# One more half chunk with the first expert layer in 44 instead of 48 short matmuls per expert

## The chip, the cores and the metric

The program runs on one core of a Trainium2 chip. The metric is the device time of one execution in microseconds (us). The engines of the core are named as the profile names them: PE (TensorE, matmuls), PEld (PE's weight loads, which overlap its matmuls), DVE (VectorE), ACT (ScalarE), POOL (GpSimd) and SP (SyncE, which here only issues DMAs). Each engine works through its own queue of instructions in order and waits for others on semaphores. PSUM is the memory that PE writes to, in eight banks.

## What is computed

A gated linear attention over 4 batches, 8 heads, 768 steps, 48 numbers per head, and behind it a mixture of 4 experts on every token (all experts are used, weighted by given probabilities):

```python
f = 1.0 / (1.0 + np.exp(-f_logit))
for t in range(S):
    state = f[:, :, t, :, None] * state + np.einsum('bhd,bhe->bhde', k[:, :, t], v[:, :, t])
    y[:, :, t] = np.einsum('bhd,bhde->bhe', q[:, :, t], state)
# x: y with the heads side by side, 3072 tokens x 384
p = domain_probs / (domain_probs.sum(-1, keepdims=True) + 1e-09)
for e in range(E):                       # 4 experts
    h = np.maximum(x @ w1[e], 0.0)       # 384 -> 1024, the first expert layer
    out += p[:, e:e + 1] * (h @ w2[e])   # 1024 -> 384, the second
```

## The kernel before

The sequence is cut into six chunks, 0 to 5, of 128 steps. In a chunk, attention is done batch by batch: from f come the gates (`gate1`, `gate2`, two activations on ACT for two batches at once from chunk 1 on), from these PE makes cumulative sums (`cs`, `pe_cs`), ACT their exponentials, DVE or POOL multiply them with q and k, a transpose follows, then PE makes the masked scores (`at`) and the output (`y`). The output is scaled by the probabilities and transposed by a DMA into `xs`, the input of the experts.

The experts of a chunk work on halves: half 0 is batches 0 and 1, half 1 batches 2 and 3, 256 tokens each. A group (chunk, half, pair) is one half through two experts. Its first layer is done in one of two ways:

- plainly (`mm_hs`): per expert 24 matmuls with 256 columns each (as long as 48 with 128 columns), 8 row blocks of 128 hidden units by 3 blocks of the 384 inputs. Four tiles of 128 x 512 leave PSUM through a ReLU on ACT or DVE (`relu_s`);
- by a Winograd form of Strassen's scheme (`l1_unit`, `mm_l1`): over two of the three input blocks, 2 x 2 blocks are multiplied with 7 products instead of 8, 28 matmuls of 128 columns, and 16 more for the third input block: 44. It needs sums of weight blocks (`u_sums`, five per expert, made once, kept in buffers that the loads of f, q, k and the gates used before) and of input blocks (`x_sum`, four per group, kept in a buffer of the loads of v), and three partial results are copied out of PSUM by ACT (`copy_l1`) and added in when a quarter of the hidden units is finished (`ev_l1`, three of four on DVE). One PSUM bank collects the four quarters one after another, so PE's next step into it waits for the eviction before.

The set `LOW` names the groups that go the second way: before the change all four of chunk 5. The second layer always goes by such a scheme: each group has seven steps of 8 matmuls with 192 columns (`mm_p`, "step 1" to "step 7" below), whose results are added to the output tile by DVE (`ev_p`). `s_sum` makes the sums of hidden blocks for them on DVE or POOL.

What stands where is not decided by the code's order. Each operation is entered with `P.add`, which gives it the next entry of the table `RANKS`: a number that is its place in the program, and at some entries a letter that fixes its engine (A for ACT, D for DVE, P for POOL). All operations are then written out in the order of these numbers, so every engine's queue, SP's queue of DMAs too, follows the table. Buffers are given out in the same order.

Two gates on loads matter below: the f of chunk 1 is loaded in two parts, and the second (`load`, `w_gate`) is issued only when a certain weight load has landed. SP issues loads, transposes and stores in one queue.

Of the kernel before, what the change touches and what calls it, by code (L numbers as in the profile page):

```python
# [143 lines left out]
def kernel(  # L144
# [957 lines left out]
    for c in range(C):  # L1102
# [30 lines left out]
        elif c > 1:  # L1133
            if c == C - 1:
                for e in sorted({2 * p + el for _, _, p in LOW for el in range(2)}):
                    u_sums(e)
# [23 lines left out]


PRINT = None
LOW = {(5, 0, 0), (5, 0, 1), (5, 1, 0), (5, 1, 1)}
BLOCKED = {(0, 1), (1, 1), (1, 3)}
YP, RP = 17, 50
B1, S1, B2, S2 = -10, 4, -2, 6
# [38 lines left out]
```

## Time and profile before

| what | value |
|---|---|
| three runs | 287.25, 286.94, 285.03 us; median 286.94 |
| the profiled execution | 285.82 us, of which the span of its instructions is 284.1 us |
| busy share of the span: PE, DVE, POOL, ACT | 97%, 73%, 65%, 63% |
| DMA | 41.88 MB, mean 147 GB/s |
| granted clock of PE | 1.00 in all but the very end |

The span runs from the first instruction to the last. The execution's time holds about 1.7 us more than the span, for what lies around it. "Busy" of PE counts matmuls from their start to a modelled end, and neighbours overlap, so that 97% does not yet say that PE never waits; the list of waits and the distances between starts do.

### The profile page before, as it was taken

The numbers are of one execution on the slowest core, as the hardware profiler recorded it, in microseconds if no ns is written. First come the engines' busy times: TensorE is split into PE (matmuls) and PEld (weight loads), VectorE is DVE, ScalarE is ACT, GpSimd is POOL, SyncE is SP. The second block draws the span as 40 slices with busy tenths as digits, with TensorE's granted clock in tenths as the row PEclk, the third lists the DMA queues.
The fourth block names the chain that finished last, engine by engine and source line by source line (L and its number), as shares of the span: only waits on it lengthen the run. The fifth ranks groups of instructions, "written<-read, shape, count | busy, mean of one in ns | idle before, by whom it ended". The sixth has DMA issues, their size and how long they took to land.

```text
span 284.1 us, 8015 instructions
## 1 busy us (share of the span) xinstructions
PE 276.0 (97%) x3228; PEld 241.2 (85%) x3228; DVE 208.7 (73%) x437; ACT 178.2 (63%) x350; POOL 185.3 (65%) x197
## 2 busy tenths in 40 slices
PE   6889999999999999999999999999999999999995
PEld 4678565668788999999998999999999899999995
DVE  5695487797779587769887786686765687857683
ACT  5668235647898848686866867769367456556420
POOL 5799353706699878667729955695656545793761
PEclk9999999999999999999999999999999999999999
DMA  6999999999988999999999999996547015201003
GB/s 156 189 195 205 208 195 200 184 216 181 162 150 159 198 164 208 204 168 184 194 175 207 194 179 218 184 166 124 111 82 160 30 31 76 67 0 59 2 2 111
DMA packets 153688, 41.88 MB, mean 147 GB/s; under 512 B 144028, under 2 KB 152860, under 8 KB 153652
## 3 DMA queue, kind: packets, MB, share of 16 engines
q1 hardware_dynamic: 142404, 34.66, 65.1%
q0 software_dynamic: 11248, 6.72, 16.8%
q8 instruction: 25, 0.41, 0.6%
q14 instruction: 11, 0.09, 0.1%
HBM read 31.51 MB, written 4.72 MB: 128 GB/s over the span
## 4 chain that ended last, share of the span: by engine, by line
PE 84%; DMA 9%; POOL 4%; ACT 1%; DVE 1%; issue 0%; ACTq 0%; POOLq 0%
PE ps_m L646 29%; PE ps_m L531 26%; PE ps_m L574 7%; DMA w_sb<-in_moe_w_dram 7%; PE ps_m L514 6%; PE ps_m L499 4%; PE ps_m L654 2%; DMA f<-in_f_logit_dram 2%; PE ps_m L437 2%; POOL w_sb L312 2%; PE ps_m L464 1%; PE ps_m L460 1%; PE ps_m L347 1%; PE ps_m L470 1%; POOL AT L441 1%; PE ps_m L362 1%
## 5 line engine op out<-in xcount | busy, mean ns | idle before, releaser
L531 PE MATMUL ps_m<-x,w_sb 128*128 128x256 bf16 x672 | 84.3, 273 | 0.0
L531 PEld LDWEIGHTS <-w_sb 128*128 128x128 bf16 x672 | 63.6, 98 | 7.1
L595 ACT ACTIVATE h<-ps_m 128x512 bf16<-128x512 f32 x82 | 46.8, 600 | 24.1 <-PE ps_m L531 23.9
L646 PEld LDWEIGHTS <-S 128*128 128x128 bf16 x576 | 48.2, 98 | 0.8
L673 DVE TENSOR_TENSOR o<-ps_m,o 128x192 f32<-128x192 f32 x91 | 31.1, 353 | 19.1 <-PE ps_m L646 17.3
L646 PEld LDWEIGHTS <-h 128*128 128x128 bf16 x432 | 36.2, 98 | 0.8
L610 POOL TENSOR_TENSOR S<-h 128x1024 bf16<-128x1024 bf16 x14 | 29.7, 2124 | 10.3 <-DVE S L610 6.3
L499 PE MATMUL ps_m<-x,w_sb 128*128 128x128 bf16 (+2 forms) x264 | 35.1, 282 | 0.0
L420 ACT ACTIVATE yb<-ps_m,pn 128x384 bf16<-128x384 f32 x55 | 29.4, 586 | 8.5 <-PE ps_m L464 5.6
L397 POOL TENSOR_TENSOR qk<-q,e 128x384 bf16<-128x384 f32 x18 | 21.6, 1201 | 12.5 <-DVE f L549 3.9
L646 PE MATMUL ps_m<-ts_sb,S 128*128 128x192 bf16 x288 | 29.3, 246 | 0.0
L646 PE MATMUL ps_m<-w_sb,h 128*128 128x192 bf16 x288 | 29.2, 246 | 0.0
L646 PE MATMUL ps_m<-w_sb,S 128*128 128x192 bf16 x288 | 28.7, 246 | 0.0
L499 PEld LDWEIGHTS <-w_sb 128*128 128x128 bf16 x264 | 21.6, 98 | 8.1
L593 DVE TENSOR_SCALAR h<-ps_m 128x512 bf16<-128x512 f32 x30 | 20.6, 688 | 9.6 <-PE ps_m L531 8.5
L453 DVE TENSOR_TENSOR AT<-ps_m,mask 128x512 bf16<-128x512 f32 x40 | 25.6, 682 | 2.1 <-PE ps_m L437 2.0
L510 ACT ACTIVATE h<-ps_m 128x512 bf16<-128x512 f32 x33 | 19.1, 595 | 12.2 <-PE ps_m L499 11.8
L380 ACT ACTIVATE e<-ps_m 128x384 f32<-128x384 f32 x40 | 23.6, 708 | 3.2 <-PE ps_m L347 1.4
L610 POOL TENSOR_TENSOR S<-h,S 128x1024 bf16<-128x1024 bf16 x10 | 21.2, 2124 | 4.5 <-DVE o L673 2.5
L514 PE MATMUL ps_m<-w_sb,h 128*128 128x384 bf16 x128 | 23.9, 326 | 0.0
L585 DVE CUSTOM_DVE_ANT_0 h<-ps_m,QK 128x512 bf16<-128x512 f32 x24 | 16.0, 686 | 5.1 <-PE ps_m L574 1.9
L588 ACT COPY QK<-ps_m 128x512 f32<-128x512 f32 x24 | 13.8, 588 | 8.1 <-PE ps_m L574 5.2
(140 smaller groups left out, 523.3 us busy)
## 6 DMA issues: line engine op xcount, KB each, us to landing
out_dram<-o SPq DMA_DIRECT2D x23, 192.0 KB, 2.5
w_sb<-in_moe_w_dram POOLq DMA_DIRECT2D x5, 768.0 KB, 15.2
k<-in_k_dram SPq DMA_DIRECT2D x10, 384.0 KB, 5.1
q<-in_q_dram SPq DMA_DIRECT2D x10, 384.0 KB, 5.0
v<-in_v_dram SPq DMA_DIRECT2D x10, 384.0 KB, 5.1
f<-in_f_logit_dram SPq DMA_DIRECT2D x9, 384.0 KB, 5.8
w_sb<-in_moe_w_dram POOLq DMA_DIRECT2D x6, 384.0 KB, 8.2
f<-in_f_logit_dram SPq DMA_DIRECT2D x6, 192.0 KB, 4.4
```

The costliest lines, as they stand in the source:

```text
L380: nc.scalar.activation(out=o, in_=i, func=AF.Exp, scale=1.0 if j else -1.0)
L397: return engines[eng].tensor_tensor(out=tl("qk", c, b)[:, j, :, 0:D].rearrange("t (i r) d -> t i r d", r=2), in0=tl("qk"[j], c, b // 2)[:, ...
L420: nc.scalar.activation(out=ys, in_=y, func=AF.Copy, scale=pe)
L453: nc.vector.tensor_tensor(out=tl("AT", c, b)[:, r].rearrange("s i t -> s (i t)"), in0=tl("A", c, b, r).rearrange("s i t -> s (i t)"), in1= ...
L499: nc.tensor.matmul(out=hp(c, e, fc, n0, n1, nf)[:, f], lhsT=w1_sb[:, e, kk, (fc + f) * 128:(fc + f + 1) * 128], rhs=tl("xT", c)[:, kk, n0: ...
L514: nc.tensor.matmul(out=tl("op", c, e, nt)[:, 0:Din], lhsT=tl("h", c, e, half_of(c, nt * T))[:, fc, nt * T:(nt + 1) * T], rhs=w2_sb[:, e, f ...
L531: nc.tensor.matmul(out=out_[:, f], lhsT=w1_sb[:, e, kk, (fc + f) * 128:(fc + f + 1) * 128], rhs=tl("xs", c, hf, p)[:, el, kk, :], start=(k ...
L593: nc.vector.tensor_relu(out=dst, in_=tl("hp", c, hf, p, el, fc))
L595: nc.scalar.activation(out=dst, in_=tl("hp", c, hf, p, el, fc), func=AF.Relu)
L610: return engines[eng].tensor_tensor(out=o, in0=in0, in1=in1, op=op)
L646: nc.tensor.matmul(out=out_, lhsT=lhs[:, f, :], rhs=rhs[:, f, :], start=(first and el == 0 and f == 0), stop=(el == 1 and f == KH - 1), sk ...
L673: nc.vector.tensor_tensor(out=o, in0=src, in1=o, op=ALU.add)
```

## The change

The groups (4, 1, 0) and (4, 1, 1), the second half of chunk 4 through both pairs of experts, join `LOW`. With them the twenty sums of weight blocks are entered at chunk 4 instead of chunk 5 (`u_sums` is called in the chunk that first needs it, and left out where the sum exists). And the table `RANKS` is another one, since 32 operations are added and every number may move: from the second expert of chunk 0 on, order and engines differ in most of the program.

```diff
 RANKS = (
-    "0 9 14 1 5 18 3 27 2 21 33 48 19 40 24 52 30 61 36 71 42 84 55 95 63 109 74 121 80 137 88 151 97 163 169 106 165 114 184 "
+    "0 9 14 1 5 18 3 27 2 21 33 48 19 40 24 52 30 61 36 71 42 84 55 95 63 109 74 121 80 137 88 151 97 163 204 106 168 114 218 "
...
         elif c > 1:
-            if c == C - 1:
-                for e in sorted({2 * p + el for _, _, p in LOW for el in range(2)}):
-                    u_sums(e)
+            for e in sorted({2 * p + el for g, _, p in LOW if g == c for el in range(2)} - {e for e, _ in usums}):
+                u_sums(e)
             for hf in range(2):
                 for p in range(NPR):
                     zip_groups((c, hf, p), prev)
...
-LOW = {(5, 0, 0), (5, 0, 1), (5, 1, 0), (5, 1, 1)}
+LOW = {(4, 1, 0), (4, 1, 1), (5, 0, 0), (5, 0, 1), (5, 1, 0), (5, 1, 1)}
```

Three places where the queues differ. The change has one line more in `RANKS`, so L499 of before is L500 after it, and so on.

PE, at the first cumulative sums of chunk 1 (the matmuls from `gp` and `Ub`; the rows on `w_sb` and `x` are the first layer of chunk 0, those on `S` are the second layer of its expert 1). Before:

```order
L654 LDWEIGHTS S_770
L654 MATMUL ps_m_711<-w_sb,S_770 128x192
L499 LDWEIGHTS w_sb
L499 MATMUL ps_m_807<-x_372,w_sb 128x512
L499 LDWEIGHTS w_sb
L499 MATMUL ps_m_807<-x_372,w_sb 128x512
L499 LDWEIGHTS w_sb
L499 MATMUL ps_m_807<-x_372,w_sb 128x512
L347 LDWEIGHTS Ub
L347 MATMUL ps_m_815<-gp_88,Ub 128x384
L347 LDWEIGHTS Ub
L347 MATMUL ps_m_818<-gp_88,Ub 128x384
```

and after the change:

```order
L500 LDWEIGHTS w_sb
L500 MATMUL ps_m_800<-x_372,w_sb 128x512
L348 LDWEIGHTS Ub
L348 MATMUL ps_m_806<-gp_88,Ub 128x384
L655 LDWEIGHTS S_681
L655 MATMUL ps_m_707<-w_sb,S_681 128x192
```

The step of the second layer that ends in the first two rows of before (step 7 of expert 1, eight matmuls) has moved behind the first cumulative sum; the other work ahead of it has the same length.

ACT, some 20 us later: the gates of a later chunk (`f<-f` is `gate1`, `gp<-f` is `gate2`), exponentials (`e`) and the ReLUs of chunk 1's first layer (`h`). Before:

```order
L334 ACTIVATE f_878<-f_878 128x768
L380 ACTIVATE e_102<-ps_m_1066 128x2x4x48
L380 ACTIVATE e_102<-ps_m_1066 128x384
L380 ACTIVATE e_104<-ps_m_1041 128x2x4x48
L380 ACTIVATE e_104<-ps_m_1041 128x384
L510 ACTIVATE h_1118<-ps_m_1081 128x2x256
L342 ACTIVATE gp_88<-f_878 128x16x48
```

and after:

```order
L335 ACTIVATE f_925<-f_925 128x768
L343 ACTIVATE gp_88<-f_925 128x16x48
L381 ACTIVATE e_104<-ps_m_1093 128x2x4x48
L381 ACTIVATE e_104<-ps_m_1093 128x384
L335 ACTIVATE f_1072<-f_1072 128x768
L511 ACTIVATE h_1150<-ps_m_1143 128x2x256
L511 ACTIVATE h_1102<-ps_m_1129 128x2x256
```

A gate of chunk 3 (`f_1072`) now stands ahead of chunk 1's ReLUs; its load is the fifth that SP issues counted from the f of chunk 2, where before the fifth was a load of k.

SP, its last stores (`o` is the output tile, 128 rows by 384 or 192 columns). Before:

```order
L677 DMA out_dram<-o_4218 128x384 x2
L677 DMA out_dram<-o_4681 128x384
L677 DMA out_dram<-o_4926 128x384
L677 DMA out_dram<-o_4681 128x384
L677 DMA out_dram<-o_4926 128x192 x2
```

and after:

```order
L678 DMA out_dram<-o_5059 128x192
L678 DMA out_dram<-o_4814 128x384
L678 DMA out_dram<-o_5059 128x192
L678 DMA out_dram<-o_5059 128x384
L678 DMA out_dram<-o_4814 128x384
```

The last store is now one of 384 columns, 192 KB, instead of one of 192 columns.

117 rows, old and new, of the table RANKS are left out of this document.

## The prediction

> **What bounds the kernel now.** I read the page first, then the list of what PE waited for, then the chain that ended last. From the page, the span and the busy shares:
>
> ```profile
> span 284.1 us, 8015 instructions
> PE 276.0 (97%) x3228; PEld 241.2 (85%) x3228; DVE 208.7 (73%) x437; ACT 178.2 (63%) x350; POOL 185.3 (65%) x197
> ```
>
> PE is busy nearly throughout. Whether it ever waits is in the list of waits on PE, over the whole span (us in total, times, longest):
>
> ```profile
> engine line waited for: us in total, times, longest us
> PE ps_m L1156 <- DVE S L192: 1.5, 1, 1.5
> PE ps_m L437 <- DVE QK L288: 1.3, 3, 0.6
> PE ps_m L464 <- POOL AT L441: 0.7, 1, 0.7
> PE ps_m L351 <- POOL mask L220: 0.7, 1, 0.7
> PE ps_m L347 <- ACT gp L342: 0.7, 1, 0.7
> ```
>
> All five belong to the start and to chunk 0's end. The same list for 50 us onward has no row at all: for 230 us PE waits for nobody. So the end is the moment of the last wait, at L347, plus the matmuls behind it, plus the tail. The chain of work shows what sets that moment (start, length):
>
> ```profile
> 41.45 5.70 DMA f<-in_f_logit_dram
> 47.24 0.85 ACT f L334
> 48.11 0.85 ACT gp L342
> ```
>
> and PE's timeline shows it standing there:
>
> ```profile
> 47.51 0.81 PE L499 MATMUL ps_m<-x,w_sb 128*128 128x512 bf16 x3
> 49.01 0.48 PE L347 MATMUL ps_m<-gp,Ub 128*128 128x384 bf16 x2 [0.68 <-ACT gp L342]
> ```
>
> Chunk 1's f is issued at 41.45 behind a weight load and lands at 47.15; two activations follow, and PE's first cumulative sum begins at 49.01. Nothing in the change makes that load earlier: SP's loads up to it and POOL's issues of weights stand in the same order.
>
> **What the half itself saves.** Two stretches of the chain give the price of a matmul of either kind, and one that of a step of the second layer:
>
> ```profile
> 88.64 0.66 PE ps_m L654 x8
> 89.47 2.62 PE ps_m L531 x24
> 256.68 2.68 PE ps_m L574 x48
> ```
>
> Plain first layer: 2.62 / 24 = 0.1092 us per matmul, 24 per expert, 2.62 us. The other form: 2.68 / 48 = 0.0558 us, 44 per expert, 2.46 us. Four expert passes (two pairs of two) change: 4 x (2.62 - 2.46) = **0.66 us less PE work**, in 284.
>
> The Trainium skill says otherwise of such short matmuls: TensorE: Matmul & The Clock Gate, section "Back-to-back issue gap", gives about 81 ns per matmul for a sustained stream of weight load and matmul with 128 columns. By it four passes would take 4 x 44 x 0.081 = 14.3 us, some 4 us more than now (an estimate from that page). The row above has a weight load per matmul as well and 55.8 ns; the trace decides.
>
> **What the new order takes back.** In the new order, step 7 of expert 1 (eight matmuls, 0.66 us by the row of x8) stands behind the first cumulative sum instead of ahead of it; the other work ahead is equal in length. PE thus arrives at the sum 0.66 us sooner, and waits for the same gate until 49.0: its wait grows from 0.68 to about 1.35. From 49.01 it works without a wait until its last step (quoted below) has gone through at 280.17 + 0.66 = 280.83, 231.8 us; after the change it still has 231.8 - 0.66 + 0.66 to do from there. The saving and the moved step cancel: **net 0.0**. If PE were late by then for another reason, up to 1.3 us of it would be covered by the same wait.
>
> **What else moves, and its cover.** The half's 16 evictions of 512 columns become 28, and eight sums of input blocks are new; the twenty weight sums are the same, only sooner. Their rows by group:
>
> ```profile
> L595 ACT ACTIVATE h<-ps_m 128x512 bf16<-128x512 f32 x82 | 46.8, 600 | 24.1 <-PE ps_m L531 23.9
> L593 DVE TENSOR_SCALAR h<-ps_m 128x512 bf16<-128x512 f32 x30 | 20.6, 688 | 9.6 <-PE ps_m L531 8.5
> L585 DVE CUSTOM_DVE_ANT_0 h<-ps_m,QK 128x512 bf16<-128x512 f32 x24 | 16.0, 686 | 5.1 <-PE ps_m L574 1.9
> L588 ACT COPY QK<-ps_m 128x512 f32<-128x512 f32 x24 | 13.8, 588 | 8.1 <-PE ps_m L574 5.2
> L561 POOL TENSOR_TENSOR v<-x,v 128x256 bf16<-128x256 bf16 x5 | 3.4, 670 | 1.6 <-DVE S L610 1.4
> ```
>
> The half had 12 evictions on ACT and 4 on DVE, 12 x 0.60 + 4 x 0.69 = 10.0 us; it gets 16 on ACT (12 copies, 4 ReLUs) and 12 on DVE, 12 x 0.59 + 4 x 0.60 + 12 x 0.69 = 17.7 us, and 8 x 0.67 = 5.4 us of input sums if all were POOL's. Spread over some 30 us they lie beside PE's matmuls:
>
> ```profile
> core 0: us, PE busy (x) PEld busy (x) DVE busy (x) ACT busy (x) POOL busy (x), PEclk, DMA share, GB/s
> 49.00:55.00 6.00, 6.00 (x48) 4.02 (x48) 4.43 (x9) 3.76 (x7) 4.30 (x6) 1.00 1.16 189
> 200.00:215.00 15.00, 15.00 (x188) 13.97 (x186) 10.67 (x24) 8.95 (x20) 9.01 (x10) 1.00 0.50 106
> 215.00:230.00 15.00, 15.00 (x178) 13.84 (x176) 9.85 (x20) 9.27 (x20) 9.19 (x7) 1.00 0.31 73
> ```
>
> In the last two of these stretches DVE has 9.5 us free in 30 and ACT 11.8, against some 5.5 and 2.3 more. The weight sums need the buffers of chunk 5's f, q and k, so SP loads these up to 25 us sooner; over the last third the DMA engines are half idle or more (0.50 and 0.31 above). I take nothing for it. If the cover were gone, each eviction that is late costs PE up to its own 0.69.
>
> The real risk is in tight pairs: two steps of the second layer into one PSUM bank with little between them. After a step's last matmul, the eviction and the next start need, by the end of the program,
>
> ```profile
> 280.17 0.82 PE L646 MATMUL ps_m<-w_sb,h 128*128 128x192 bf16 x8
> 281.03 0.36 DVE L673 TENSOR_TENSOR o<-ps_m,o 128x192 f32<-128x192 f32 x1 [0.30 <-PE ps_m L646]
> ```
>
> 0.16 (the end beyond its 0.66) + 0.04 + 0.36, and 0.05 until PE goes on (48.96 to 49.01 above): 0.61 us. Adding up the PE steps that stand between such pairs, the closest before the change had 1.11 us; after it five have less, the closest (chunk 2, half 0, pair 0, steps 7 and 4) 0.81. All clear 0.61 if DVE is free at that moment; if a 0.69 operation is just running, up to 0.5 us is lost. Bounds: 0 and 5 x 0.5 = 2.5; I take **0.3**, near the lower end, since the chains of other kinds (scores to output, ReLU to sums) keep their closest distances (2.16 and 2.17 us for scores to output).
>
> The last store: the two last ones (96 KB) landed in the first of these rows' time, all five of the end in the second:
>
> ```profile
> DMA to landing us min/median/max: 1.6/1.6/1.6
> ...
> DMA to landing us min/median/max: 1.6/1.8/1.9
> ```
>
> A 192 KB store at the very end lands 1.9 - 1.6 = **0.3 us** later; bounds 0 and, by the page's medians of 2.5 and 1.6, 0.9.
>
> **Sum.** 284.1 - 0.66 + 0.66 + 0.3 + 0.3 = 284.7 of span. The profiled execution took 285.82, 1.72 above its span, so 286.4; the median of the runs shown is 286.94, 1.1 above that, which would give 287.5. I take the middle, **287.0**.
>
> **The rivals.**
> (a) The saving stays: the load of f happens to land sooner, or PE is late enough to use the wait. Then 0.66 less, 286.3. For it: only that DMA landings vary. Against: the same queue ahead of it.
> (b) ACT is held up by chunk 3's gate. It now stands ahead of four ReLUs of chunk 1, and waits for the load that SP issues as fifth after the f of chunk 2's start. That place in the old queue was a load of k:
>
> ```profile
> 62.69 1.61 SPq L301 DMA_DIRECT2D k<-in_k_dram  x1
> ...
> f<-in_f_logit_dram SPq DMA_DIRECT2D x9, 384.0 KB, 5.8
> ```
>
> so it lands near 62.7 + 5.8 = 68.5. Summed from 49.0, PE's second layer wants the first of these ReLUs at 73.6 and the fourth at 74.3 (an estimate: the new order's steps at the rates above); a gate and four ReLUs take 0.85 + 4 x 0.60 + 0.2 = 3.45. It decides from a landing at about 70.8 on, and every us beyond costs PE one: three late would make 290. For it: the load moved ahead into the busiest stretch for DMA (a share of 1.16 from 49 to 55, above). Against: 2.3 us of room.
> (c) DVE, which by the letters of `RANKS` gets 14 operations more (the half's 12 evictions at 0.69 among them, some 9 us in all), is the engine that the tight pairs run into; a dozen pairs have under 1.4 us, at up to 0.5 each some 3 us more, 290. Against: 9.5 us of 30 free even in the changed half.
> (d) Matmuls of 128 columns slow down when the half runs amid chunk 4's other work, toward the 81 ns named above: some 4 us more, 291. Chunk 5's rows say no.
> (e) The change does not do what it says: excluded as far as the order goes, 176 matmuls of 128 columns stand where 96 of 256 stood.
>
> **How the numbers follow.** A measurement of this kernel tells about 1%, 2.9 us, from no change; its own runs spread over 2.2. Forecast 0.66, (a) 0.12, (b) 0.08, (c) 0.12, (d) 0.01, 0.01 for a gain by luck in the start. Only (b), (c) and (d) can reach slower by over 1%, and half of (c)'s smaller forms stay below; with something for delays in a reordered program that I don't see, slower 0.18. Faster by over 1% has no source: all waits of PE together are 4.9 us and lie where the order is nearly unchanged; 0.02. Within 1%: 0.80. The range runs from 285.0, the lowest run shown, which (a) would reach on a good day, to 290.0, where (b) and (c) at their middle end.
>
> **What would show it.** In the list of waits on PE, L348 (the sum's new line) should stand with 1.2 to 1.5 us instead of 0.7, starting near 48.35 and ending at 49.0; behind 50 us there should be no row, or rows of a few tenths at L647. The groups should show 352 + 176 matmuls of 128 columns at 219 ns each and 56 ns apart, and 576 instead of 672 at the plain form. The last store should land 1.8 to 1.9 after its issue. I am wrong if PE's first sum of chunk 1 starts elsewhere than at 49.0, or if waits for DVE or ACT of more than 1 us in all stand behind it.

## The result

In 22 runs of each kernel the median is 288.47 us after the change (286.97 to 293.79) and 286.31 us before (285.03 to 291.46). The ratio of after to before is 1.0077, with a 95% interval of 1.0049 to 1.0105: slower by 0.8%, less than the 1% that the prediction called a difference. Here and below the ratios leave out single slow runs (three of after, 292.24 to 293.79, one of before, 291.46, and one of 997.30 in "banks kept"), while the medians are over all runs. The forecast was 287.0, the range 285.0 to 290.0. The profiled execution took 288.16 us, with a span of 286.4; before it was 285.82 and 284.1. These 2.3 us of span can be found one by one.

From the page of the kernel after, the span and the busy shares:

```profile
span 286.4 us, 8192 instructions
PE 275.4 (96%) x3308; PEld 240.9 (84%) x3308; DVE 216.3 (76%) x451; ACT 180.3 (63%) x355; POOL 183.0 (64%) x198
```

PE is busy 0.6 us less, as the shorter half should have it, and the span is longer all the same. What PE waited for, from 45 us to the end (us in total, times, longest); before there was one row here, 0.7 us at the first cumulative sum:

```profile
PE ps_m L348 <- ACT gp L343: 2.1, 2, 1.8
PE ps_m L647 <- ACT e L381: 0.6, 1, 0.6
PE ps_m L532 <- DMA x<-yb: 0.2, 1, 0.2
```

PE's timeline at these places, with the matmuls ahead of each (start, length):

```profile
49.21 0.32 PE L348 MATMUL ps_m<-gp,Ub 128*128 128x384 bf16 x1 [1.81 <-ACT gp L343]
...
66.83 0.82 PE L500 MATMUL ps_m<-x,w_sb 128*128 128x256 bf16 x6
67.98 0.32 PE L348 MATMUL ps_m<-gp,Ub 128*128 128x384 bf16 x1 [0.34 <-ACT gp L343]
...
115.27 1.24 PE L647 MATMUL ps_m<-ts_sb,S 128*128 128x192 bf16 x13
116.71 1.49 PE L532 MATMUL ps_m<-x,w_sb 128*128 128x256 bf16 x12 [0.21 <-DMA x<-yb]
...
138.47 0.82 PE L532 MATMUL ps_m<-x,w_sb 128*128 128x256 bf16 x6
139.93 0.82 PE L647 MATMUL ps_m<-ts_sb,S 128*128 128x192 bf16 x8 [0.64 <-ACT e L381]
...
282.17 0.82 PE L647 MATMUL ps_m<-w_sb,h 128*128 128x192 bf16 x8
```

A group's length ends 0.16 us after the moment at which the next matmul could have started, so the loss is larger than the bracket. Six matmuls of 256 columns take 0.65 us at PE's steady rate, a step of eight 0.66; measured against that, PE is late by 0.50 at 67.98 (cs 2.1, a cumulative sum of chunk 2), by 0.37 at 116.71 (first layer of group (2, 0, 1): chunk 2, half 0, pair 1) and by 0.80 at 139.93 (second layer of that group, step 5): **1.67 us**. Behind 140 us PE waits for nobody, and there lie the changed half and all of the experts of chunk 5.

The account: the first sum begins at 49.21 instead of 49.01 (+0.20). From it to the end of the last step PE takes 282.17 + 0.66 - 49.21 = 233.62 us instead of 231.82 (+1.80, of which 1.67 are the three waits and 0.13 are spread). The tail behind it is 3.53 instead of 3.28 (+0.25; in hundredths the spans are 286.36 and 284.11). Together 2.25.

The chain of work of the kernel after shows what released the wait at 67.98 and the two later ones:

```profile
41.42 5.64 DMA f<-in_f_logit_dram
47.44 0.85 ACT f L335
48.45 10.57 DMA v<-in_v_dram
59.58 1.55 POOL ts_sb L633
61.13 3.54 DMA egs<-e
64.75 1.20 ACT e L381 x2
66.31 0.75 ACT f L335
67.09 0.85 ACT gp L343
...
113.41 3.25 DMA x<-yb
116.71 1.49 PE ps_m L532 x12
...
134.02 0.94 POOL qk L398
134.96 3.67 DMA egs<-e
139.93 0.82 PE ps_m L647 x8
```

Read the first piece downwards: v of chunk 1 lands at 59.0; POOL, which has stood before the cast of v, does the cast and a sum of weight blocks and only then issues a transfer of 2 KB, `egs` (the decay factors of a chunk, moved out of the exponentials' buffer `e`). It lands 3.5 us later. ACT's next exponentials need that buffer, the gate of chunk 2 stands behind them, and PE's sum behind the gate. At 139.93 it is the same kind of transfer: an exponential on ACT waits until `egs` has left the buffer, and with the exponential the PSUM bank that step 5 is to have. At 116.71 it is a transpose on SP's queue.

What these transfers waited for is not their data. For the first of them the order of two loads matters. The f of chunk 1 comes in three loads: batch 0, batch 1 (the gated one, which opens the first sum) and batches 2 and 3 together. Before, SP issued v of chunk 1 (batches 0 and 1) ahead of that third f; now it is the other way round. SP's queue and the instructions that waited, before:

```profile
47.09 1.45 SPq L301 DMA_DIRECT2D v<-in_v_dram  x1
48.64 5.94 SPq L301 DMA_DIRECT2D f<-in_f_logit_dram  x2
...
59.20 0.84 ACT L334 ACTIVATE f<-f 128x768 f32<-128x768 f32 x1 [2.67 <-DMA f<-in_f_logit_dram]
```

and after:

```profile
47.02 1.39 SPq L302 DMA_DIRECT2D f<-in_f_logit_dram  x1
48.45 1.80 SPq L302 DMA_DIRECT2D v<-in_v_dram  x1
...
59.08 0.50 POOL L289 CAST vb<-v 128x384 bf16<-128x384 f32 x1 [2.39 <-DMA v<-in_v_dram]
59.54 1.64 POOL L633 TENSOR_TENSOR ts_sb<-w_sb 128x768 bf16<-128x768 bf16 x1
61.13 0.62 POOL L391 DMA_DIRECT2D egs<-e  x1
...
59.04 0.51 ACT L288 CAST vb<-v 128x384 bf16<-128x384 f32 x1 [3.43 <-DMA v<-in_v_dram]
59.46 0.84 ACT L335 ACTIVATE f<-f 128x768 f32<-128x768 f32 x1
```

The load issued second lands at 59, whichever it is. Before, that was f, which only the gate needed; after, it is v, for which POOL and ACT both stand still, with work behind them that does not need v. No run puts these two loads back in their old order, so how much that alone is worth is not shown. (The profile puts POOL's 0.62 beside `egs` and the chain 3.54. The Trainium skill, Perfetto Trace Analysis, "DMA Instruction — SWDGE (GPSIMD)", says that the profiled end of a DMA issued by POOL is the end of making its descriptors and not of the move; the trace agrees, 61.75 against a landing at 64.67.)

The changed half itself, its matmuls in both forms and the additions that grew with it:

```profile
L532 PE MATMUL ps_m<-x,w_sb 128*128 128x256 bf16 x576 | 72.1, 272 | 0.2 <-DMA x<-yb 0.2
L575 PE MATMUL ps_m<-x,w_sb 128*128 128x128 bf16 x240 | 23.4, 219 | 0.0
L586 DVE CUSTOM_DVE_ANT_0 h<-ps_m,QK 128x512 bf16<-128x512 f32 x36 | 24.0, 687 | 10.7 <-PE ps_m L575 7.3
```

576 plain matmuls instead of 672, durations as before, and no idle time of PE at the short ones.

### The profile page after: what moved, and what is told of

The parts are those of the page before. It is cut to its first block, busy times and chain, and to the rows that moved or that the text cites. A ratio compares the mean times of both kernels' runs of the same rounds, so it can differ in the third digit from the quotient of the medians.

```text
span 286.4 us, 8192 instructions
## 1 busy us (share of the span) xinstructions
PE 275.4 (96%) x3308; PEld 240.9 (84%) x3308; DVE 216.3 (76%) x451; ACT 180.3 (63%) x355; POOL 183.0 (64%) x198
## 4 chain that ended last, share of the span: by engine, by line
PE 69%; DMA 18%; POOL 6%; DVE 2%; issue 2%; ACT 2%; SPq 1%; ACTq 0%; POOLq 0%; DVEq 0%
PE ps_m L647 26%; PE ps_m L532 20%; PE ps_m L575 10%; DMA w_sb<-in_moe_w_dram 7%; DMA v<-in_v_dram 4%; PE ps_m L500 3%; DMA egs<-e 3%; POOL w_sb L313 2%; PE ps_m L515 2%; DMA f<-in_f_logit_dram 2%; PE ps_m L655 2%; DMA k<-in_k_dram 1%; PE ps_m L438 1%; POOL vb L294 1%; PE ps_m L465 1%
## 5 line engine op out<-in xcount | busy, mean ns | idle before, releaser
L532 PE MATMUL ps_m<-x,w_sb 128*128 128x256 bf16 x576 | 72.1, 272 | 0.2 <-DMA x<-yb 0.2
L532 PEld LDWEIGHTS <-w_sb 128*128 128x128 bf16 x576 | 54.7, 98 | 6.3 <-DMA x<-yb 0.4
L596 ACT ACTIVATE h<-ps_m 128x512 bf16<-128x512 f32 x69 | 39.6, 599 | 23.8 <-PE ps_m L532 21.0
L611 POOL TENSOR_TENSOR S<-h 128x1024 bf16<-128x1024 bf16 x17 | 36.0, 2126 | 8.9 <-DVE S L611 5.8
L500 PE MATMUL ps_m<-x,w_sb 128*128 128x128 bf16 (+2 forms) x264 | 34.7, 282 | 0.7 <-DMA w_sb<-in_moe_w_dram 0.7
L421 ACT ACTIVATE yb<-ps_m,pn 128x384 bf16<-128x384 f32 x56 | 31.0, 588 | 4.3 <-PE ps_m L465 2.1
L586 DVE CUSTOM_DVE_ANT_0 h<-ps_m,QK 128x512 bf16<-128x512 f32 x36 | 24.0, 687 | 10.7 <-PE ps_m L575 7.3
L589 ACT COPY QK<-ps_m 128x512 f32<-128x512 f32 x36 | 20.9, 589 | 15.2 <-DVE h L586 6.7
L500 PEld LDWEIGHTS <-w_sb 128*128 128x128 bf16 x264 | 21.6, 98 | 9.9 <-DMA w_sb<-in_moe_w_dram 1.0
L611 POOL TENSOR_TENSOR S<-h,S 128x1024 bf16<-128x1024 bf16 x7 | 14.9, 2130 | 15.0 <-ACT QK L589 10.1
L398 POOL TENSOR_TENSOR qk<-q,e 128x384 bf16<-128x384 f32 x16 | 19.0, 1195 | 8.4 <-DVE S L611 2.8
L511 ACT ACTIVATE h<-ps_m 128x512 bf16<-128x512 f32 x30 | 17.5, 596 | 10.5 <-PE ps_m L500 10.2
L575 PE MATMUL ps_m<-x,w_sb 128*128 128x128 bf16 x240 | 23.4, 219 | 0.0
```

The source lines that it names most:

```text
L421: nc.scalar.activation(out=ys, in_=y, func=AF.Copy, scale=pe)
L500: nc.tensor.matmul(out=hp(c, e, fc, n0, n1, nf)[:, f], lhsT=w1_sb[:, e, kk, (fc + f) * 128:(fc + f + 1) * 128], rhs=tl("xT", c)[:, kk, n0: ...
L532: nc.tensor.matmul(out=out_[:, f], lhsT=w1_sb[:, e, kk, (fc + f) * 128:(fc + f + 1) * 128], rhs=tl("xs", c, hf, p)[:, el, kk, :], start=(k ...
L575: nc.tensor.matmul(out=out_[:, f], lhsT=lhs[:, f * 128:(f + 1) * 128], rhs=rhs, start=(step in "125" and f == 0 and i == 0), stop=(i == le ...
L586: return nc.vector._custom_dve(dve_ops.TENSOR_ADD_SAT, out=dst, in0=src, in1=add, s0=float("inf"), s1=0.0)
L596: nc.scalar.activation(out=dst, in_=tl("hp", c, hf, p, el, fc), func=AF.Relu)
```

## The experiments

The theory after this reading: the half and the moved step do what the prediction said, and the loss is three transfers that the new order put behind work they do not need. The rival: the half's added evictions and sums cost it, and the waits would come elsewhere without these. Nearly all edits only move operations (in the runs that keep the PSUM banks, a table also names the bank of every tile). `MOVE` gives an operation of `P.add` a rank between two of the table's:

```diff
-        op.prio = int(rank.rstrip("ADP"))
+        op.prio = MOVE.get(op.name, int(rank.rstrip("ADP")))
```

All profiles in one table. "First sum" is its start and the wait there; "late" is PE's delay against its steady rate behind it, where over 0.15; "to the end" goes from the first sum's start to the end of the last step; times in us.

| kernel | span | first sum | late, behind the first sum | to the end | median | ratio to before |
|---|---|---|---|---|---|---|
| before | 284.1 | 49.01 (0.68) | none | 231.8 | 286.31 | |
| after | 286.4 | 49.21 (1.81) | 0.50, 0.37, 0.80 | 233.6 | 288.47 | 1.0077 [1.0049, 1.0105] |
| step 7 back | 286.5 | 48.46 (0.70) | kv 1.0 1.35, 0.46, 1.26, 0.34 | 234.6 | 288.05 | 1.0065 [1.0038, 1.0092] |
| three transfers ahead | 284.0 | 48.71 (1.16) | none | 231.8 | 286.65 | 1.0022 [1.0000, 1.0043] |
| both | 283.6 | 48.35 (0) | kv 1.0 0.23 | 231.7 | 286.85 | 1.0032 [1.0006, 1.0057] |
| both, second profile | 285.2 | 48.82 (0.9) | kv 1.0 1.26, 0.43 | 232.9 | | |
| both, third profile | 285.4 | 49.11 (0) | kv 1.0 1.46 | 232.8 | | |
| half undone | 288.8 | 48.89 (1.88) | 0.84, 1.88, 0.87, 0.28 | 236.4 | 289.17 | 1.0125 [1.0077, 1.0173] |
| before, one step late | 284.1 | 48.29 (0.48) | none | 232.5 | 285.87 | 0.9997 [0.9974, 1.0020] |
| both, margins | 285.4 | 49.01 (0.4) | kv 1.0 1.31, 0.31 | 232.9 | 286.55 | 1.0025 [0.9991, 1.0060] |
| both, banks kept | 284.5 | 48.98 (0.6) | cs 1.3 0.32, 0.33 | 232.0 | 286.33 | 1.0027 [0.9999, 1.0054] |
| and ReLU ahead | 286.8 | 48.85 (0.7) | cs 1.3 1.12, 1.25, 0.34, 0.20 | 234.4 | 286.83 | 1.0040 [1.0010, 1.0071] |
| and cast behind gate | 284.2 | 49.00 (0) | 0.45 | 231.7 | 286.44 | 1.0025 [0.9994, 1.0055] |
| all | 284.3 | 49.05 (0) | 0.29, 0.20 | 231.7 | 285.95 | 0.9997 [0.9960, 1.0034] |

The ratios go by the runs of before on the same chip, whose medians were 285.55 to 286.31. The kernel after was timed only with the result, and not again beside the later runs.

### The three transfers ahead

```diff
+MOVE = {"egs 1.0": 278.5, "xs 2.0.1": 588.5, "egs 3.0": 712.5}
```

> The kernel after, with three operations moved in their queues, all of them transfers that stood behind something that they don't need: on POOL the decay factors of chunk 1, batch 0 ahead of a weight sum (they had been ready since 51.8 and were issued at 61.1) and those of chunk 3, batch 0 ahead of those of batch 2 (ready since 110.9, issued at 135.0), on SP the transpose xs 2.0.1 ahead of a store (ready since 99.1, issued at 113.4). Theory (the time went to these three waits): 0.50 at cs 2.1, 0.37 at the first layer of chunk 2's pair 1 and 0.80 at step 5 of chunk 2's pair 1 go, 1.67 us in all, span 284.7 to 285.0. Rival (the loss is spread over the half's added evictions and sums, and these waits would be made up anyway): span within 0.4 of 286.4.

The list of waits behind 45 us has one row left:

```profile
PE ps_m L348 <- ACT gp L343: 1.2, 1, 1.2
```

The span is 284.0, 2.4 shorter (0.5 of it because f landed sooner), the three waits are gone, and none came in their place. From the first sum to the end PE takes 280.52 - 48.71 = 231.81 us, as before to 0.02. The theory expected 284.7 to 285.0, which with those 0.5 is what came; the rival falls. The timed runs agree: the ratio goes from 1.0077 to 1.0022, 1.6 us less, and the two intervals do not meet. What remains at the median, 0.2%, this profile does not show, as its execution (285.83) was 0.8 faster than the median one. That the way to the end is again that of before fits the prediction's central claim, that the half's 0.66 and step 7's 0.66 cancel.

The edit has a side effect. `Plan.run` hands out PSUM banks in the order of the ranks, and with these three moves 44 PSUM tiles get another bank, all of them behind the first two waits, but step 5's among them. Which of the two ended the wait at step 5 is settled by the run "banks kept" below: there step 5 has the bank that it has in the kernel after, the transfers are moved, and it does not wait.

### Step 7 back

```diff
+MOVE = {"p 0.d1.7": 239.5}
```

> The kernel after, with one step moved: the second layer's step 7 of expert 1, chunk 0 (eight matmuls, 0.66 us), back ahead of chunk 1's first cumulative sum. By the prediction's reason the wait at that sum shrinks from 1.8 to about 1.15 us and everything behind starts 0.66 sooner against the same work. But the theory has a second gate behind it: the cumulative sum cs 2.1 at 68.0 waits for a chain that starts with the landing of v at 59.0 (POOL's cast, a weight sum, the small transfer of the decay factors, 3 us to land, an exponential on ACT), and none of that knows of PE. So its wait should grow from 0.50 to about 1.15 and the end stay: span 286.3 to 286.5, no gain. Rival (only the order at the first sum matters): the end comes 0.66 sooner, span 285.7.

The wait at the first sum shrank as expected and the end did not move: 286.5. So the gain is eaten behind it. But the place was another one:

```profile
61.42 0.33 PE L471 MATMUL ps_m<-vb,qk 128*128 128x96 bf16 x4 [1.20 <-ACT h L511]
```

This is `kv 1.0` (the key and value sum of chunk 1, batch 0), ahead of cs 2.1, and it waits for a ReLU on ACT. Here too banks changed: moving step 7 gave kv 1.0 the bank of a tile of chunk 0 (h 0.3.4) whose ReLU stands on ACT behind the cast of v. That a later wait would eat the gain was right; the wait that was named, cs 2.1, is not late in this profile, and step 5 waits 1.26 instead of 0.80.

### Both

> Both edits of the two runs before together. Theory: with the second gate gone, the 0.66 of step 7 comes through as well, 286.4 - 1.67 - 0.66 = 284.1 of span, as the kernel before (284.1), or up to 0.3 less if the wait at step 5 hid more. Rival of spread losses: still within 0.4 of 286.4. If the moved step is worth nothing: 284.7.

283.6 in the profile, the shortest of all, but the median is 286.85, no better than the three transfers alone. The profiled execution was its luckiest. Hence two more profiles of the same kernel:

> The kernel with both edits (four operations moved), once more and alone for its profile: its profiled execution before was the shortest of its twelve (283.6 of span, the middle one 285.0) and showed no wait of PE behind 45 us. Theory of thin margins: in that profile four of PE's steps began less than 0.7 us after the landing of the DMA transpose that they need (0.14, 0.36, 0.45 and 0.67 us), where the kernel before had two (0.44, 0.86); landings of the same queue differ by more than that, so an execution of 284.5 or more should show waits of PE for such a transpose, 0.3 to 1.5 us in all. Rival (the rest is in the start, before 49 us, or in the tail): no such rows, and the first cumulative sum later than 48.9.

> The same kernel and the same two readings as in the look before it: waits for transposes where the span is 284.5 or more (thin margins), or a late first cumulative sum or tail (rival).

Both spans are over 284.5, and neither shows a wait for a transpose, nor are the first sum or the tail late: both expectations fall. It is kv 1.0 again, late by 1.26 and 1.46. In the lucky execution v had landed at 57.5, in these at 59.0 and 59.5:

```profile
62.19 0.33 PE L471 MATMUL ps_m<-vb,qk 128*128 128x96 bf16 x4 [1.30 <-ACT h L511]
...
59.52 0.51 ACT L288 CAST vb<-v 128x384 bf16<-128x384 f32 x1 [4.63 <-DMA v<-in_v_dram]
...
61.56 0.58 ACT L511 ACTIVATE h<-ps_m 128x512 bf16<-128x512 f32 x1
```

(the third profile; ACT idles 4.6 us for v with the gate's two activations and a finished tile's ReLU behind it).

### The half undone

`LOW` as before, with plain matmuls, 24 per expert, on the places of the short ones; everything else, the early weight sums too, as after. Of the edit only `LOW` is shown; `u_sums` is still entered at chunk 4, and the table is written for the shorter list. SP's queue is that of after, and until the scores of chunk 5 the banks are too.

```diff
-LOW = {(4, 1, 0), (4, 1, 1), (5, 0, 0), (5, 0, 1), (5, 1, 0), (5, 1, 1)}
+LOW = {(5, 0, 0), (5, 0, 1), (5, 1, 0), (5, 1, 1)}
```

> The kernel after, with its order, its early weight sums and its early loads, but the half itself undone: the four expert passes by 24 matmuls of 256 columns each, on the places of the short ones, 12 evictions on ACT and 4 on DVE as before, no sums of input blocks. Theory (the half saves what its matmuls save, the loss sits far ahead of it): PE has 4 x 0.16 = 0.66 us more, the three waits stay, span 287.0, time up by 0.2% against after. Rival (the half's added evictions and sums cost the 2 us): the loss goes, span 284.5 to 285.

```profile
PE ps_m L347 <- ACT gp L342: 2.6, 2, 1.9
PE ps_m L531 <- DMA x<-yb: 1.7, 1, 1.7
PE ps_m L646 <- ACT e L380: 0.7, 1, 0.7
```

The loss does not go: the same three places wait, long before the half, the transpose even 1.88 instead of 0.37 (why so much longer is not shown), so that the span is 288.8 and not 287.0. Without the waits behind the first sum the way to the end is 236.38 - 3.87 = 232.51 us; for the kernel after it is 233.62 - 1.67 = 231.95. The half saves 0.56 by that, against 0.66 worked out. The ratio to before is 1.0125, above the 1.0077 of after, though from six runs only, and the two intervals overlap.

### One step late, in the kernel before

The converse. Step 7 itself cannot stand behind the sums here, as the operations that evict it come ahead of that place; so another step of the same length (h 0.2.5) goes behind the first two sums, with all PSUM tiles in the banks they had.

```diff
+MOVE = {"h 0.2.5.0": 245.1}
```

> The kernel before, its PSUM banks unchanged, with one 0.66 us step of PE's work (h 0.2.5, first layer of expert 2, chunk 0) behind chunk 1's first two cumulative sums instead of ahead of them. The prediction's term: the wait there grows from 0.7 to 1.3 us and the end comes 0.66 later, since no second gate stood close behind it: span 284.8, the median 0.5 to 0.7 up. Rival (a later wait has room for it, or the place is worth nothing): within 0.2 of 284.1.

From the first sum to the end 232.53 instead of 231.82: +0.71, the expected term. But in this execution the gate was open at 48.2, 0.7 sooner, and the span is 284.1; the ratio to before is 0.9997, with an interval from -0.7 to +0.6 us that neither confirms the 0.5 to 0.7 nor excludes them. The term is shown in the profile and not in the time.

### Margins, banks, ReLU, cast

Five operations of SP's queue later:

```diff
+"store 0.0.0": 470.6, "ld v2.2": 470.5, "ld k3.0": 556.5, "ld v3.0": 564.5, "store 1.0.0": 795.5
```

> Both edits, and on SP's queue five operations moved back that nobody waits for at once (two stores, and loads of v and k used 3 to 8 us after their landing), so that the transposes behind them are issued 0.6 to 2.4 us sooner: xs 1.3.1, xs 2.0.0, tp 2.2 and 2.3, xs 3.0.0 and 3.1.0. Theory of thin margins: the profile as with both edits (span 283.4 to 284.0, little to gain where no wait stood), but the median of the timed executions falls by 0.5 to 1.0 to 286.0, level with the kernel before or below. Rival (the 1 us between the profile and the median has another cause): the median stays at 286.8.

The median hardly falls (286.55) and kv 1.0 waits 1.31 as before: so the wait that stands there is not one for a transpose, and that thin margins keep the median up is not shown. Next, both edits with every PSUM tile in the bank that it has in the kernel after:

> Both edits (four operations moved), with every PSUM tile in the bank that it has in the kernel after. Moving step 7 alone had also changed which tiles share banks, and the key and value sum kv 1.0 (at 61 to 62 us) then got the bank of h 0.3.4, whose ReLU stands on ACT behind a cast that waits for v: it waited 1.3 to 1.5 us in three of four profiles. Theory (that bank is what kept the median at 286.8): no wait at kv 1.0, span 283.5 to 284.1 in the middle execution and not only in the best, median 285.3 to 285.8. Rival (the ReLU behind the cast is late for whoever has its bank): a wait of about 1 us at cs 1.3, the next owner, median near 286.6.

kv 1.0 no longer waits, as the theory had it, and neither does step 5, in its bank of after. The next owner of the bank, cs 1.3, is late by 0.32: the rival's place, but less than its 1 us. The median, 286.33, is between both. Then the ReLU ahead of the cast:

```diff
+"relu 0.3.4.0": 281.5
```

> As the run with the banks kept, and on ACT the ReLU of h 0.3.4 ahead of the cast of v 1.0 instead of three operations behind it: ACT stood idle there for 3 to 4 us, and the ReLU's matmuls had been done since about 53 us. Both theories (bank or ReLU) expect no wait of PE between 50 and 280 us that is over 0.4: span 283.2 to 284.0, median 285.2 to 285.7, so level with the kernel before (whose median was 285.7 to 285.9 on these chips) or 0.1 to 0.5 ahead. If the median stays at 286.6, the cause is not on PE's waits in this stretch.

A miss for both theories. v landed at 59.9 in this execution, and cs 1.3 waited for the gate that also stands behind the cast:

```profile
62.09 0.48 PE L348 MATMUL ps_m<-gp,Ub 128*128 128x384 bf16 x2 [0.95 <-ACT gp L343]
...
59.91 0.51 ACT L288 CAST vb<-v 128x384 bf16<-128x384 f32 x1 [4.80 <-DMA v<-in_v_dram]
```

and the transpose xs 2.0.0, issued at 101.0 and landed at 105.5, held PE for 1.25 us: a thin margin after all. (The list of waits names DVE there, whose eviction ended 0.08 after the landing. But the weight load that follows begins 0.10 us after the landing, and so it does in "banks kept" and "cast behind gate", where that eviction ended at other times.) So the cast itself was moved, behind gate and ReLU:

```diff
+"v 1.0": 301.5
```

> Both edits with the PSUM banks of after, and on ACT the cast of v 1.0 behind chunk 1's second gate (gate1 1.2, gate2 1.2) and the ReLU of h 0.3.4 instead of ahead of them. In all nine profiles of the new order ACT stood idle for 3 to 5 us at that cast, until v landed at 57.5 to 59.9, although f for the gate had landed at 51 to 52: the two loads have changed places on SP's queue, and the one issued second lands 7 us later. Theory (this cast is what remains): gate2 1.2 ends near 57 instead of 60.6 to 62.0, no wait of PE at kv 1.0 or cs 1.3 in any execution, span 283.2 to 284.4, median 285.3 to 285.9, level with the kernel before. Rival (the remaining loss is in later thin margins, such as the transpose xs 2.0.0 at 103 to 105 us): the waits at 61 us go, and the median stays at 286.3 to 286.8.

The waits at 61 us are gone, and the gate's second activation ends at 56.4 instead of 61.2:

```profile
55.55 0.84 ACT L343 ACTIVATE gp<-f 128x768 bf16<-128x768 f32 x1
56.30 0.58 ACT L511 ACTIVATE h<-ps_m 128x512 bf16<-128x512 f32 x1
58.94 0.51 ACT L288 CAST vb<-v 128x384 bf16<-128x384 f32 x1 [2.06 <-DMA v<-in_v_dram]
```

The span is 284.2 but the median 286.44: the rival's number. The chain of work of this execution no longer passes through f or v at all:

```profile
10.71 7.61 DMA w_sb<-in_moe_w_dram
18.36 1.30 PE ps_m L500 x12
```

From there it is PE all the way. The first sum begins at 49.00 without a wait, though its gate was open at 48.4: PE itself came late, and step 7's 0.66 ahead of the sum is then paid again. That limits what any edit of this kind can win.

Last, all of it with the five moves on SP and the store of 96 KB last of all:

```diff
+"p 5.1.1.3": 1585.5, "ev_p 5.1.1.3": 1586.5, "store 5.2.192": 1587.5
```

> As the run before it, with the five operations of SP's queue moved back as in the run for margins, and with the last steps of PE in another order (the step whose store has 96 KB last, the one whose store has 192 KB ahead of it). Theories: the tail from the end of the last step falls from 3.6 to 3.3 us; if the transposes' margins matter as well, the median falls below the run before by more than that 0.3, to 284.9 to 285.5, faster than the kernel before by 0.1 to 0.3%; if not, by 0.3 alone.

The median is 285.95, level with the kernel before (0.9997). It is 0.5 below the run before it, more than the 0.3 of the tail, but not down to the 285.5 that the margins should give, and the intervals of the two runs overlap: whether the margins matter is not shown. No version was measurably faster than before.

The tail did not shrink: 3.6. The last stores, issue to landing (least, median and most of four, as the very last has no landing in any profile; before: 1.6, 1.8 and 1.9, the row in the prediction), first of the kernel after, then here, then with the half undone:

```profile
DMA to landing us min/median/max: 1.7/2.2/2.8
```

```profile
DMA to landing us min/median/max: 2.0/3.1/3.4
```

```profile
DMA to landing us min/median/max: 1.6/1.7/1.9
```

Before, the five issues stand within 4.1 us (277.3 to 281.4), in these three within 3.0 to 3.1. That they are close together does not make the tail by itself, as the half undone shows: its stores land as fast as before's, and its tail is 3.5 all the same. The size of the last store fits better: the eleven profiles that end with 192 KB have 3.50 to 3.54, the two of the old order, with 96 KB last, 3.28 and 3.29. Against it stands this run alone, 96 KB last and 3.6, with the other four stores slower than in any other profile (2.0 to 3.4). What makes the tail stays open.

## Why the prediction was right, and where not

- **What bounds the kernel, and the gate.** Right for the first sum: it began at 49.21 (predicted 49.0), still released by the gated f and two activations. That PE would wait for nobody behind it, as before, was carried over to a new order and did not hold.
- **What the half saves (0.66).** Right: 0.56 by the half undone. The way to the end with the three transfers moved, equal to before's to 0.02, fits a saving as large as the moved step.
- **What the new order takes back (0.66).** Right as a term: the wait grew to 1.81, 0.66 by the step, 0.20 by a later gate, and PE was there 0.27 sooner than that. (The sentence that the wait would start near 48.35 was a slip: that is where it started before; 1.35 ahead of 49.0 is 47.65, measured 47.40.) One step late in the kernel before cost 0.71. "Net 0.0" held, as far as single profiles show.
- **What else moves, and its cover.** The step that failed. Evictions and input sums were hidden, as said. The tight pairs, priced at 0.3, cost nothing: no wait for DVE behind 45 us. What is missing is a term for the transfers that the new order moved in chunks 1 to 3. The prediction looked at the loads for chunk 5 ("I take nothing for it") and at one load of chunk 3, and gave the rest a part of a chance, "delays in a reordered program that I don't see". But v and f of chunk 1 changed places, two transfers of 2 KB and a transpose got behind work that they do not need, and that is 1.67 us. The share of the DMA engines says nothing on who stands behind whom. The prediction's own sign of being wrong, over 1 us of waits for DVE or ACT behind the first sum, stands at its edge: the two waits for ACT are 0.34 and 0.64 by the brackets, 0.50 and 0.80 against PE's steady rate.
- **The last store (0.3).** The size was right, 3.53 against 3.28; the reason, 192 KB instead of 96, fits all profiles but the last run's and stays open. Its first row, "the two last ones", is the landing of one store, as the very last has none.
- **Sum.** 284.7 predicted, 286.4 measured: + 1.67 for the waits, + 0.20 for the gate, + 0.13 spread, - 0.3 for the pairs, - 0.05 for the tail. From the span to the forecast, luck helped. The 287.0 stands 0.6 above the 286.4 of the sum because the median of before was 286.94 in three runs; over 22 runs it is 286.31. Against before, the forecast was no change and the measured one 2.2 us, yet the time is only 1.5 above 287.0.
- **The rivals.** (a) did not come: the gate was not sooner. (b) named the right stretch and engine, ACT at 60 to 70 us held by a load, but the wrong load: the f of chunk 3 landed at 68.2 (68.5 estimated) and delayed nobody, while v of chunk 1, 9 us ahead of it, did. (c) did not come: no wait for DVE stands behind 45 us. (d) did not come: the chain of the kernel after has

```profile
224.65 1.34 PE ps_m L575 x24
251.33 4.02 PE ps_m L575 x72
```

55.8 ns per short matmul, in the changed half (first row) and in chunk 5 (second), not the 81 that the Trainium skill gives (TensorE: Matmul & The Clock Gate, "Back-to-back issue gap"). (e) did not come: 576 plain matmuls are left, as worked out.
- **Chances.** Within 1% had 0.80, and 0.8% came, close to the limit (the interval reaches 1.05%); the range's upper part, put there for (b), (c) and delays not seen, is where the time fell.

## What to carry to other kernels

When a table of places is made anew, list for every queue the transfers that changed places, and for each when its data were ready and what it now stands behind; a 2 KB transfer behind work that it does not need cost 0.50 us at one place and 0.80 at another here, where the edit itself saves 0.66. An engine that waits in order at an operation with a late input holds all that stands behind it, so look at who is queued there, not at how busy the engine is. And a gain ahead of a fixed gate counts only up to the wait at that gate, and three executions of one kernel ("both") show that wait as 0, 0.9 and 0.

## What was not expected of the hardware

- Two loads of 384 KB issued 1.4 to 1.6 us apart landed 6.3 to 8.1 us apart, in both orders: issued at 46 to 47 us, landed at 51 to 52; issued at 47.5 to 48.6, landed at 57.5 to 59.9 in the twelve profiles of kernels with the new order, and at 57.8 and 59.2 in the two with the old. Why the second takes 10.6 us where the median of such loads is 5.2 was not tried. In all fourteen profiles a weight load of 768 KB, issued by POOL 0.6 to 0.7 us behind it, landed 0.4 to 1.3 us ahead of it, and SP's next load took 10.0 to 12.0 us too; that these three held one another up is likely from this, and not shown.
- A transfer of 2 KB from buffer to buffer, issued by POOL, takes 2.0, 3.1 and 4.9 us from issue to landing (least, median and most of 16 in the kernel after), where the median of a load of 384 KB is 5.2.
- Executions differ by when the same gate opens: the first sum's gate at 48.3, 48.8 and 49.0 in the three profiles of one kernel ("both"), at 48.2 to 49.2 over all profiles. Differences under 1 us between two single profiles mean nothing without the row of that gate beside them.
